# A recurrent attention and a three-branch MLP in one program: chunks 0 to 3 select on VectorE alone, clears after the warming operand's, weight loads after x's copies, and another order of the first part's attention steps

## The chip, the cores and the metric

The program runs on one core of one Trainium2 chip. Time is device time in microseconds (us); where several runs are given, their median counts. Profiled rows come from one execution, whose own time is given below.

## What is computed

The reference, cut to what matters (batch 4, 8 heads, 768 tokens, head size 48; the MLP has model size 384 and inner size 768; the four MLP weights arrive as 64-bit floats):

```
for t in range(S):
    cur = einsum('bhd,bhe->bhde', u[None] * k[t], v[t])
    y[t] = einsum('bhd,bhde->bhe', r[t], state + cur)
    state = w[t][..., None] * state + einsum('bhd,bhe->bhde', k[t], v[t])
x = y.transpose(0, 2, 1, 3).reshape(3072, 384)
h = maximum(maximum(x @ w1, x @ w2), x @ w3)
out = h @ w_out
```

## The kernel before

**Tiling.** Each of the 4 sequences is cut into 6 chunks of 128 tokens, 24 chunks in all, numbered k. Four chunks make a half of 512 tokens, which is one tile `x` of the MLP, 6 halves in all. A guard at the end (`judge`, a flag, a slow general program behind a branch) covers inputs for which the fast form is not exact; it plays no part here.

**Attention steps.** `steps` (line 574) names each step of a chunk with a letter; a string of such letters with chunk numbers is the order in which every engine gets its instructions, since the schedule is manual and each engine runs its list in order:

- n: load `tin` (w, r, k, u of a chunk, L250) on SP. b, s, f, r: backward scan (VectorE, L357) and a copy of its ends (ScalarE, L359), reciprocal (L365), forward scan (L370), products that scale k and r (L381, L382). c: a guard's square (ScalarE, L387).
- d, D, e: the diagonal. For chunks 0 to 5 VectorE multiplies r and k (L395), TensorE sums against u (L408), ScalarE copies the sums (`cs`, L421). Then for chunks 0 and 1 ScalarE writes eight scaled identities into the weight tile `a` (L429), for the others GpSimd selects them in (L432). From chunk 6 on the product is GpSimd's (L398, L399) and the sum VectorE's (L423). e also issues the next chunk's `v` and `kr` loads on SP (L237, L238).
- X: scores into the PSUM tile `gram` (L453). N: `take_full`, ScalarE copies the third block of `gram` to `a` (L464). M: `take`, VectorE copies the other two blocks under a mask (L468). O: `take_alone`, VectorE does both (L472, then L468).
- T, U, S, R: transposed k (L483, copied to `kn` by ScalarE, L485), state update (L506, L510), its scaling (ScalarE L522 for chunks 0 to 3, VectorE L519 and L525 later), the state's share of y (L496).
- V, Z: the two groups of value products into `y` (L545). E: ScalarE copies `y` into `x` (L563); for the third and fourth chunk of the first half, and for the last chunk of any later half, six small copies within `x` follow (`x<-x`, L572), three on SP and three on ScalarE's queue in the first half, all six on SP later.

**MLP.** `moe_groups` yields groups. A half has 18 input groups (6 blocks f of the inner size, 3 branches) and 8 output groups of three matmuls 128x384 each. In the first half the first 6 input groups are plain fp32 products against weights 0 to 5 (`psm<-x,wh`; the first two are begun on 384 tokens, L149, and finished on 128, L157), and the other 12 take three fp32r products each (`x_hi,wh`, `x_lo,wh`, `x_hi,wl`, L169); its output groups are plain (L189). `take_up` drains each PSUM tile: ScalarE copies the first branch (L132), VectorE takes the maximum with the other two (L135). Three PSUM tiles serve the groups.

**Weights.** There are 24 weight tiles. `load_w` loads one as raw 64-bit words (384 KB, L306, SP, six raw buffers). `begin` casts the top part on ScalarE (`split_w1`, L313) and first loads until `NST` tiles are ahead of the cast; `weights` (letter c) joins the parts on VectorE (`split_w2`, L320); `fix` (letter f) splits a weight into a high part on ScalarE (L112) and a low part on VectorE (L113).

**Order.** `FRONT` (line 72) is the order of the opening: attention steps of chunks 0 to 3 and parts of 4, with W (warming matmuls on a tile `warm`, L594), w (one weight load), i (a cast), p and m (an MLP group), c, x, y (splitting x). `START` (line 80) follows: m is a group, a is one unit of the attention strings `TURN` and `ORD` (a chunk has 6 units; the first of a chunk holds R, V, U, the next chunk's X, Z and E), c a weight, f a split. It ends with the first input group of the second half. After it a loop keeps groups and units in step, which is unchanged. Before all, `warmer(WARM)` issues ten warming matmuls; GpSimd clears three `top` tiles (L287) before it clears `warm` (L589).

```
def take_alone(k):
    to, data = views(k)
    nc.vector.tensor_copy(out=to[:, :, 2, :], in_=data[:, :, 2, :])
    take(k)
...
while loaded < min(NW, begun + (NST if groups else 1)):
    load_w()
```

Of the kernel before, what the change touches and what calls it, by code (L numbers as in the profile page):

```python
# [62 lines left out]
GPH = 3 * FT + 2 * CPH  # L63
UPC = 6
UPH = UPC * CPH
NST = 4
WARM = 10
XD, LEAD = -2, 0

FRONT = ("b0 s0 f0 d0 W2 D0 W3 r0 X0 N0 e0 T0 W3 c0 b1 s1 d1 D1 U0 f1 W2 R0 e1 S0 M0 V0 Z0 E0 n3 r1 "
# [3 lines left out]
TURN = "b1 d1 w | f1 w | D1 r1 c1 | e1 M0 w | "  # L76
ORD = "w R0 V0 U0 X1 Z0 E0 N1 b2 d2 | f2 n3 w | D2 S0 r2 c2 | e2 M1 w | T1 w | |"


START = ("mcyamcyfamcyffamcfamcfamcfamcfamcfamcfamcfamcfamcfamcfcamccamccamaamaamaamafafaxmafmmammaaf")  # L80
CS = 6
EARLY = 2
LINE = 128
# [12 lines left out]
def kernel(ctx: ExitStack, tc, tin, nat, u_flat, u_pair, v_t, w_all, out, ytr):  # L96
    nc = tc.nc
# [107 lines left out]
    with ExitStack() as fast:  # L205
# [77 lines left out]

        stage = {}
        tops = [cst.tile([128, PC], U32, name=f"top{i}") for i in range(3)]
        for t in tops:
            nc.gpsimd.memset(t[:, :], 0)  # L287

        loaded = 0

# [5 lines left out]
        def load_w():  # L296
            nonlocal loaded
            if loaded == NW:
                return
            i, loaded = loaded, loaded + 1  # L300
            if w_all.dtype == F32:
                place(i)
                nc.sync.dma_start(out=wval[i], in_=w_all[i])
                return
            raw = raw_p.tile([128, lines(2 * PC + 1)], I32, name="raw")
            nc.sync.dma_start(out=raw[:, :].bitcast(U16)[:, 1:4 * PC + 1], in_=w_all[i].bitcast(U16))  # L306
            stage[i] = raw
# [271 lines left out]
        def ahead(step, k):  # L579

            if k < NK and (step, k) not in ready:
                ready.add((step, k))
                steps[step](k)
# [3 lines left out]
            nc.vector.tensor_copy(out=ident2[lo:lo + HC, :], in_=ident[lo:lo + HC, lo:lo + HC])  # L587
        warm = cst.tile([128, 128], BF16, name="warm")
        nc.gpsimd.memset(warm[:, :], 0.0)  # L589

        def warmer(n):
            wps = ps_m.tile([128, HT], F32, name="psm")
            for _ in range(n):
                nc.tensor.matmul(wps[:, :], lhsT=warm[:, :], start=True, stop=True,  # L594
                                 rhs=warm[:, :].unsqueeze(1).broadcast_to([128, HT // 128, 128]))
# [49 lines left out]
        def begin():  # L645

            nonlocal begun
            while loaded < min(NW, begun + (NST if groups else 1)):
                load_w()
# [74 lines left out]
        def take_x(early=False):  # L724
            h = len(xs)
            there = ("E", CPH * (h + 1) - 2) in ready if early else units >= min(UPH * (h + 1) + XD, UPC * NK)
            if h < NH and there and groups >= GPH * h - 2 * CPH:
                x_parts(h)
# [43 lines left out]
        simple = dict(p=part, a=unit, c=weights, i=begin, w=load_w, m=group, f=fix, y=x_next, x=lambda: take_x(True))  # L772
        for step in FRONT.split():
            if step in simple:
# [3 lines left out]
            else:  # L778
                ahead(step[0], int(step[1:]))
        for step in START:  # L780
            simple[step]()
# [7 lines left out]
    with tc.If(verdict[0] != 0, label="general"), ExitStack() as slow:  # L789
        pool = lambda name, bufs, **kw: slow.enter_context(tc.tile_pool(name=name, bufs=bufs, **kw))  # L790
        c1 = pool("c1", 1)
# [83 lines left out]
        with tc.For_i(0, NH) as half:  # L875
            x = xs_p.tile([128, KT, HT], F32, name="x")
# [73 lines left out]
```

## Time and profile before

| what | us |
|---|---|
| median of 3 runs | 419.01 |
| lowest and highest run | 413.47, 419.7 |
| the profiled execution's time | 419.3 |
| its span, first to last instruction | 417.5 |

A row of a timeline gives start, duration, engine, line, operation, output and inputs, and a count; what stands in brackets is the engine's idle time before it and what ended that. Rows with a count merge neighbours. PEclk is the granted clock of TensorE as a share of its full 2.4 GHz, so 0.50 is 1.2 GHz. Weight loads into TensorE (PEld) overlap its matmuls.

### The profile page before, as it was taken

The page shows a single profiled execution, that of the slowest core. Times are in us where ns is not written, and L with a number is a line of the kernel's source. Part 1 is how long each engine was busy: PE and PEld are TensorE (multiplying, and loading weights), DVE is VectorE, ACT ScalarE, POOL GpSimd, SP SyncE. Part 2 cuts the span into 40 slices and gives each one's busy share as a digit, 9 for nine tenths or more (in the row PEclk, how much of TensorE's full clock was granted, in tenths as well). Part 3 has the DMA queues.
Part 4 walks back from the last instruction along what each step waited for, and adds up shares of the span by engine and source line. Part 5 has one row for each costly group of instructions (what it writes and reads, how often), then busy time and mean ns, then how long its engine had stood idle before and what let it go on. Part 6 is the DMA issues. An engine that isn't in the chain of part 4 may idle for free.

```text
span 417.5 us, 9220 instructions
## 1 busy us (share of the span) xinstructions
PE 400.6 (96%) x3762; PEld 325.6 (78%) x3762; DVE 251.2 (60%) x437; ACT 179.1 (43%) x406; POOL 82.0 (20%) x95
## 2 busy tenths in 40 slices
PE   5899899999699999999999999999999999999995
PEld 2666558776387888988889988888988888978894
DVE  7666789989637776547758558667636523223310
ACT  1744674844424323447447656545623321412211
POOL 3030104324221213321312311321321300000000
PEclk9769999999989999999999999999999999999998
DMA  8544888671361303190312280430470000300002
GB/s 223 168 147 139 252 320 276 188 228 42 86 203 36 125 5 121 50 289 6 125 57 68 61 271 14 147 102 0 111 233 3 2 2 0 96 1 2 0 1 79
DMA packets 20814, 44.65 MB, mean 107 GB/s; under 512 B 2944, under 2 KB 9536, under 8 KB 20768
## 3 DMA queue, kind: packets, MB, share of 16 engines
q1 hardware_dynamic: 20160, 43.34, 33.3%
q10 hardware_dynamic: 608, 0.69, 0.6%
q8 instruction: 30, 0.49, 0.5%
q14 instruction: 16, 0.13, 0.1%
HBM read 38.12 MB, written 4.72 MB: 103 GB/s over the span
## 4 chain that ended last, share of the span: by engine, by line
PE 82%; DVE 6%; DMA 4%; ACT 3%; issue 2%; POOL 1%; ACTq 1%; SPq 0%; POOLq 0%; DVEq 0%
PE psm L169 47%; PE psm L189 17%; PE gram L453 4%; PE y L545 4%; PE tu L506 3%; PE y L496 3%; DMA raw<-in_w_all_dram 2%; PE psm L594 2%; PE tu L483 2%; DMA x<-x 2%; DVE wl L113 1%; DVE wl L320 1%; DVE h_hi L135 1%; DVE tin L381 1%; PE psm L408 1%
## 5 line engine op out<-in xcount | busy, mean ns | idle before, releaser
L169 PE MATMUL psm<-x_hi,wh 128*128 128x512 f32 x306 | 122.7, 401 | 3.5 <-ACT m L200 3.2
L169 PE MATMUL psm<-x_hi,wl 128*128 128x512 f32 x306 | 120.1, 393 | 0.7 <-DVE wl L113 0.7
L169 PE MATMUL psm<-x_lo,wh 128*128 128x512 f32 x306 | 119.9, 392 | 0.0
L135 DVE TENSOR_TENSOR m<-psm,m 128x512 f32<-128x512 f32 x60 | 41.5, 691 | 74.0 <-PE psm L169 62.3
L169 PEld LDWEIGHTS psm<-x_hi,wh 128*128 128x128 f32 x306 | 57.8, 189 | 16.9 <-ACT m L200 3.9
L169 PEld LDWEIGHTS psm<-x_hi,wl 128*128 128x128 f32 x306 | 57.8, 189 | 13.7 <-DVE wl L113 1.5
L169 PEld LDWEIGHTS psm<-x_lo,wh 128*128 128x128 f32 x306 | 57.9, 189 | 11.4 <-DVE x_lo L113 0.2
L432 POOL TENSOR_SCALAR_AFFINE_SELECT a<-cs 64x512 f32<-64x512 f32 x44 | 31.6, 718 | 138.3 <-DVE cs L423 52.1
L189 PE MATMUL psm<-wl,h_hi 128*128 128x384 f32 x168 | 56.5, 379 | 0.0
L398 POOL TENSOR_TENSOR kr<-kr 128x384 f32<-128x384 f32 x18 | 25.0, 1391 | 109.4 <-PE y L545 101.4
L563 ACT COPY x<-y 112x512 f32<-112x512 f32 x24 | 14.1, 586 | 68.2 <-PE y L545 68.2
L189 PE MATMUL psm<-wh,h_hi 128*128 128x384 f32 x120 | 41.0, 342 | 0.0
L189 PE MATMUL psm<-wh,h_lo 128*128 128x384 f32 x120 | 40.2, 335 | 0.0
L112 ACT CAST h_hi<-m 128x512 fp32r<-128x512 f32 x30 | 18.7, 622 | 47.9 <-DVE m L135 47.9
L189 PEld LDWEIGHTS psm<-wl,h_hi 128*128 128x128 f32 x168 | 31.4, 189 | 5.6
L387 ACT ACTIVATE gf<-gf 112x1034 f32<-112x1034 f32 x24 | 25.6, 1068 | 22.3 <-DVE tin L382 22.3
L113 DVE TENSOR_TENSOR h_lo<-m,h_hi 128x512 fp32r<-128x512 f32 x30 | 20.7, 690 | 21.8 <-ACT h_hi L112 21.8
L357 DVE TENSOR_TENSOR_SCAN gf<-tin,d_bwd 112x517 f32<-112x517 f32 x24 | 30.6, 1274 | 3.7 <-DMA tin<-in_tin_dram 3.7
L370 DVE TENSOR_TENSOR_SCAN gf<-tin,d_fwd 112x517 f32<-112x517 f32 x24 | 31.7, 1320 | 0.7
L545 PE MATMUL y<-a,v 64*48 64x64 f32 (+3 forms) x768 | 26.4, 256 | 0.8
L545 PEld LDWEIGHTS y<-a,v 64*64 64x64 f32 (+1 forms) x768 | 22.4, 132 | 4.7 <-issue 1.8
L113 DVE TENSOR_TENSOR x_lo<-x,x_hi 128x512 fp32r<-128x512 f32 x18 | 11.6, 689 | 22.6 <-ACT x_hi L112 22.6
(87 smaller groups left out, 508.0 us busy)
## 6 DMA issues: line engine op xcount, KB each, us to landing
tin<-in_tin_dram SPq DMA_DIRECT2D x23, 448.0 KB, 4.6
raw<-in_w_all_dram SPq DMA_DIRECT2D x24, 384.0 KB, 5.7
kr<-in_nat_dram SPq DMA_DIRECT2D x18, 384.0 KB, 4.9
tin<-in_tin_dram SPq DMA_DIRECT2D x23, 231.0 KB, 2.9
v<-in_nat_dram SPq DMA_DIRECT2D x24, 192.0 KB, 4.7
out_dram<-m SPq DMA_DIRECT2D x23, 192.0 KB, 2.1
x<-x SPq DMA_DIRECT2D x30, 32.0 KB, 2.0
tin<-in_tin_dram SPq DMA_DIRECT2D x1, 256.0 KB, 4.8
```

Source lines behind the costliest of these rows:

```text
L112: nc.scalar.copy(out=hi, in_=src)
L113: rest = lambda: nc.vector.tensor_tensor(out=lo, in0=src, in1=hi.bitcast(F32), op=ALU.subtract)
L135: nc.vector.tensor_tensor(out=m[:, :], in0=ps[:, :], in1=m[:, :], op=ALU.max)
L169: nc.tensor.matmul(ps[:, :], lhsT=wt[f * 3 + wi][:, ct * 128:(ct + 1) * 128], rhs=xt[:, ct, :], start=(n == 0), stop=(n == KT * len(terms) ...
L189: nc.tensor.matmul(pss[tt][:, 0:DM], lhsT=ht[f][:, tok], rhs=wt[FT * 3 + f][:, :], start=(f == 0 and i == 0), stop=(f == FT - 1 and i == l ...
L357: nc.vector.tensor_tensor_scan(out=gf[0:112, 0, ::-1], data0=t[0:112, 0:WC][:, ::-1], data1=d_bwd[0:112, ::-1], initial=0.0, op0=ALU.mult, ...
L370: nc.vector.tensor_tensor_scan(out=gf[0:112, 1, :], data0=tbuf[k % NB][0:112, 0:WC], data1=d_fwd[0:112, :], initial=0.0, op0=ALU.mult, op1 ...
L387: nc.scalar.activation(out=flat, in_=flat, func=AF.Square, accum_out=acc[0:112, k:k + 1])
L398: nc.gpsimd.tensor_tensor(out=n[:, 0, :], in0=n[:, 0, :], in1=n[:, 1, :], op=ALU.mult)
L432: nc.gpsimd.affine_select(out=a[rows, 0:2, :, :], pattern=[[0, 2], [0, 4], [1, HC]], in_=cs[rows, :].rearrange("p (a b) -> p a b", a=2).un ...
L453: nc.tensor.matmul(to, lhsT=p["kp"][q:q + 48, pr, lo:lo + HC], rhs=p["rp"][q:q + 48, pr, HC * late:C], start=(hh, lo) not in begun, stop=T ...
L545: mm = nc.tensor.matmul(p["y"][64 * half:64 * half + m, hh, j, HC * late:C], lhsT=natt[k][0][lo:lo + HC, h * D:h * D + m], rhs=a[:, j, :] ...
```

## The change

Chunks 0, 1 and 2 get O where they had N and M, as chunk 3 had already: VectorE does both copies, and ScalarE's copy (L464) is gone for them. Two weight loads (w w) move from behind E2 to behind E3. `NST` goes from 4 to 3. The three clears of `top` follow the clear of `warm` on GpSimd. `START` has the same number of groups (24), units (28) and weights (18), in another order: units come earlier among the three-product groups, so that the second half's x is written seven output groups ahead of its first product and not four; two more splits (f) stand in it, 19 for 17.

```
-NST = 4
+NST = 3
-FRONT = ("b0 s0 f0 d0 W2 D0 W3 r0 X0 N0 e0 T0 W3 c0 b1 s1 d1 D1 U0 f1 W2 R0 e1 S0 M0 V0 Z0 E0 n3 r1 "
-         "W1 X1 N1 d2 D2 e2 w w T1 c1 b2 s2 R1 U1 S1 M1 V1 Z1 E1 f2 r2 "
-         "W4 X2 N2 d3 D3 e3 w n4 w T2 c2 b3 s3 R2 U2 S2 i i M2 V2 Z2 E2 w w f3 r3 "
-         "W3 X3 T3 i R3 O3 x V3 Z3 E3 n5 U3 p p d4 w c n6 w m D4 b4 s4 c c3 S3 m w f4 c e4 m r4 c X4 N4 T4 R4 c4 w w")
+FRONT = ("b0 s0 f0 d0 W2 D0 W3 r0 X0 e0 T0 W3 c0 b1 s1 d1 D1 U0 f1 W2 R0 e1 S0 O0 V0 Z0 E0 n3 r1 "
+         "W1 X1 d2 D2 e2 w w T1 c1 b2 s2 R1 U1 S1 O1 V1 Z1 E1 f2 r2 "
+         "W4 X2 d3 D3 e3 w n4 w T2 c2 b3 s3 R2 U2 S2 i i O2 V2 Z2 E2 f3 r3 "
+         "W3 X3 T3 i R3 O3 x V3 Z3 E3 w w n5 U3 p p d4 w c n6 w m D4 b4 s4 c c3 S3 m w f4 c e4 m r4 c X4 N4 T4 R4 c4 w w")
-START = ("mcyamcyfamcyffamcfamcfamcfamcfamcfamcfamcfamcfamcfamcfcamccamccamaamaamaamafafaxmafmmammaaf")
+START = ("mcyamcyfamcyffamcfamcfamcfaamcfamcfaamcfamcfaamcfamcfaamcfamccaamccamcaaamfamfmfamxfamamfmamf")
...
         tops = [cst.tile([128, PC], U32, name=f"top{i}") for i in range(3)]
-        for t in tops:
-            nc.gpsimd.memset(t[:, :], 0)
...
         nc.gpsimd.memset(warm[:, :], 0.0)
+        for t in tops:
+            nc.gpsimd.memset(t[:, :], 0)
```

In the changed program the lines from 288 to 589 stand two lines higher, so that L470 below is L472 of before, L466 is L468, L570 is L572 and so on.

VectorE, chunk 0's selection and chunk 1's preparation, before:

```order
L370 SCALAR_TENSOR_TENSOR gf<-tin_118,d_fwd 112x517
L468 COPY_PREDICATED a<-mask,gram 128x2x2x128
L381 TENSOR_TENSOR tin_118<-tin_118,gf 112x2x128 x2
L382 TENSOR_TENSOR tin_118<-tin_118,gf 112x512
L395 TENSOR_TENSOR kr<-tin_119 112x2x128 x2
```

The same place now:

```order
L368 SCALAR_TENSOR_TENSOR gf<-tin_118,d_fwd 112x517
L470 COPY a<-gram 128x256
L466 COPY_PREDICATED a<-mask,gram 128x2x2x128
L379 TENSOR_TENSOR tin_118<-tin_118,gf 112x2x128 x2
L380 TENSOR_TENSOR tin_118<-tin_118,gf 112x512
L393 TENSOR_TENSOR kr<-tin_119 112x2x128 x2
```

One copy is added on VectorE ahead of the selection, and nothing else moves; chunks 1 and 2 have the same.

SP's queue at the end of the first half's attention, from chunk 4's `tin` (n4, tin_118) to chunk 5's (tin_119), before:

```order
L250 DMA tin_118<-in_tin_dram 112x528
L306 DMA raw<-in_w_all_dram 128x1536
L572 DMA x<-x 16x384 x3
L306 DMA raw<-in_w_all_dram 128x1536 x2
L572 DMA x<-x 16x128 x3
L250 DMA tin_119<-in_tin_dram 112x528
```

The same place now:

```order
L250 DMA tin_118<-in_tin_dram 112x1024
L304 DMA raw<-in_w_all_dram 128x1536
L570 DMA x<-x 16x384 x3
L570 DMA x<-x 16x128 x3
L304 DMA raw<-in_w_all_dram 128x1536 x2
L250 DMA tin_119<-in_tin_dram 112x528
```

Weights 4 and 5 now stand behind both sets of x's copies.

TensorE from the last value products of chunk 7 (they end the second half's x) to the second half's first product, before:

```order
L545 MATMUL y<-a,v 64x64
L545 MATMUL y<-a,v 48x64
L189 MATMUL psm<-wl,h_hi 128x384 x12
L169 MATMUL psm<-x_hi,wh 128x512
L169 MATMUL psm<-x_lo,wh 128x512
```

The same place now:

```order
L543 MATMUL y<-a,v 64x64
L543 MATMUL y<-a,v 48x64
L189 MATMUL psm<-wl,h_hi 128x384 x15
L481 MATMUL tu<-ident,tin_119 128x112 x4
L189 MATMUL psm<-wl,h_hi 128x384 x6
L169 MATMUL psm<-x_hi,wh 128x512
```

Twenty-one output matmuls (seven groups) stand there now, where twelve (four groups) stood.

## Rows read from the trace of the kernel before

**Rows 1.** The page's first part: busy time, share of the span, instructions of each engine.

```profile
PE 400.6 (96%) x3762; PEld 325.6 (78%) x3762; DVE 251.2 (60%) x437; ACT 179.1 (43%) x406; POOL 82.0 (20%) x95
```

**Rows 2.** The chain that ended last, in order of time: start, us, what.

```profile
2.97 1.08 POOL top L287 x3
...
140.08 8.39 PE psm L169 x36
```

**Rows 3.** Timeline of TensorE alone, 0 to 50 us.

```profile
14.22 0.67 PE L506 MATMUL tu<-v,kn 128*64 128x48 f32 x16 [1.29 <-ACT kn L485]
...
17.84 1.56 PE L453 MATMUL gram<-tin 48*64 48x128 f32 x32
...
27.89 1.34 PE L453 MATMUL gram<-tin 48*64 48x128 f32 x32
...
33.96 0.90 PE L453 MATMUL gram<-tin 48*64 48x128 f32 x32
...
38.40 4.04 PE L149 MATMUL psm<-x,wh 128*128 128x384 f32 x12
...
43.54 1.07 PE L157 MATMUL psm<-x,wh 128*128 128x128 f32 x6 [1.10 <-DMA x<-x]
...
45.10 0.94 PE L157 MATMUL psm<-x,wh 128*128 128x128 f32 x6
...
48.54 0.90 PE L453 MATMUL gram<-tin 48*64 48x128 f32 x32
```

**Rows 4.** Stretches: length, busy time by engine (x instructions), PEclk, DMA share, GB/s.

```profile
15.50:28.50 13.00, 12.76 (x171) 9.05 (x174) 8.27 (x14) 6.80 (x24) 2.28 (x2) 0.50 0.34 105
64.24:78.96 14.72, 14.45 (x122) 11.51 (x123) 14.65 (x27) 8.32 (x18) 4.29 (x4) 1.00 0.70 220
115.00:120.00 5.00, 5.00 (x20) 3.99 (x19) 1.06 (x1) 1.90 (x4) 0.00 (x0) 0.74 0.72 236
```

**Rows 5.** VectorE's groups from 0 to 39 us: busy us, mean ns, idle before.

```profile
L357 DVE TENSOR_TENSOR_SCAN gf<-tin,d_bwd 112x517 f32<-112x517 f32 x5 | 6.1, 1229 | 1.5 <-DMA tin<-in_tin_dram 1.5
L370 DVE TENSOR_TENSOR_SCAN gf<-tin,d_fwd 112x517 f32<-112x517 f32 x4 | 5.1, 1268 | 0.0
L381 DVE TENSOR_TENSOR tin<-tin,gf 112x256 f32<-112x256 f32 x8 | 4.3, 573 | 0.0
L395 DVE TENSOR_TENSOR kr<-tin 112x256 f32<-112x256 f32 x10 | 3.7, 412 | 0.0
L468 DVE COPY_PREDICATED a<-mask,gram 128x512 f32<-128x512 int32 x4 | 2.9, 732 | 7.8 <-ACT a L464 5.9 <-ACT a L429 1.8
L382 DVE TENSOR_TENSOR tin<-tin,gf 112x512 f32<-112x512 f32 x4 | 2.7, 684 | 0.0
...
L472 DVE COPY a<-gram 128x256 f32<-128x256 f32 x1 | 0.4, 425 | 1.5 <-PE gram L453 1.5
```

**Rows 6.** Timeline of all engines, round chunk 7's y and the second half's first product.

```profile
103.05 8.01 PE L189 MATMUL psm<-wl,h_hi 128*128 128x384 f32 x24
...
114.30 0.79 PE L169 MATMUL psm<-x_hi,wh 128*128 128x512 f32 x1 [3.24 <-ACT m L200]
```

**Rows 7.** Timeline of all engines, 10 to 45 us: VectorE, SP's queue and ScalarE.

```profile
10.77 1.23 DVE L370 TENSOR_TENSOR_SCAN gf<-tin,d_fwd 112x517 f32<-112x517 f32 x1
...
34.56 1.86 SPq L572 DMA_DIRECT2D x<-x  x3
...
42.21 0.62 ACT L313 CAST top<-raw 128x384 f16<-128x384 bf16 x1
```

**Rows 8.** The tile `raw` from 0 to 60 us: issue of a weight load to its landing.

```profile
DMA to landing us min/median/max: 3.5/6.3/8.4
```

**Rows 9.** VectorE's groups from 64.24 to 78.96 us.

```profile
L113 DVE TENSOR_TENSOR wl<-wl,wh 128x384 fp32r<-128x384 f32 x7 | 5.1, 730 | 0.0
L320 DVE SCALAR_TENSOR_TENSOR wl<-raw,top 128x384 uint32<-128x384 uint32 x6 | 3.7, 616 | 0.0
L135 DVE TENSOR_TENSOR h_hi<-psm,h_hi 128x512 f32<-128x512 f32 x4 | 2.7, 669 | 0.0
```

## The prediction

> **What bounds the kernel now.** I read the page first, then the chain that ended last in order of time, then TensorE's own timeline, stretches with the granted clock, and VectorE's groups. The page says that TensorE is busy 96% of the span and VectorE 60% [rows 1]. From about 118 us on the chain is TensorE's groups one behind another, 36 fp32r matmuls in 8.39 us [rows 2], that is 2.10 us for a group of nine; the change leaves these groups as they are. So a gain must come from the part before. There the reader is to see four places.
>
> First, the scores of chunks 1, 2 and 3 start at 17.84, 27.89 and 33.96 us [rows 3]: 10.05 us from the one to the next, then 6.07. In the long gap TensorE works at 0.50 of its clock, 1.2 GHz, for 13 us on end [rows 4], and not long before that it had stood still 1.29 us for `kn` [rows 3]. VectorE meanwhile loses 7.8 us in front of its masked copies, waiting for ScalarE's copy (5.9) and for the diagonals (1.8) [rows 5]. Second, TensorE waits 1.10 us for x's second set of copies at 43.54 [rows 3]. Third, from 64.24 to 78.96 both engines are full: TensorE 14.45 and VectorE 14.65 of 14.72 us [rows 4]. Fourth, the second half's first product comes at 114.30 after 3.24 us of idle time [rows 6], and then the clock shows 0.74 in 115 to 120 [rows 4].
>
> **The change part by part.** The sum is made against the profiled execution's 419.3 us (span 417.5); the median of the runs is 419.01, so the two agree to 0.3.
>
> *The clears.* The three clears of `top` take 1.08 us ahead of the warming operand [rows 2]. Behind it, the warming matmuls end about 1.1 us sooner. VectorE's scans set what comes next, so I count nothing; GpSimd's next work is chunk 2's selection, and the clears' first reader is the first weight's cast, both far later. Without that cover it would be 1.1 us, either way.
>
> *N and M become O.* ScalarE loses three copies, VectorE gains three of 0.43 us. With ScalarE's copy gone from the front of its queue, the eight scaled identities of chunk 0 follow the diagonal's sum at once and are done before VectorE is, so VectorE runs without the 7.8 us of waits. By durations [rows 5] one chunk costs it 1.23 and 1.27 (scans), 2 x 0.57 and 0.68 (products), 2 x 0.41 (diagonal), 0.43 and 0.73 (selection): 6.3 us. Its forward scan of chunk 1 starts at 10.77 and takes 1.23 [rows 7], so it is free at 12.0. Selecting chunk 0 (1.16) and scaling chunk 1 (1.83) gives the scores of chunk 1 at 15.0; one round later those of chunk 2 at 21.3, and those of chunk 3 at 27.6, against 33.96: 6.4 us sooner. TensorE must do a chunk in 6.3 us for that. It did one in 6.07 at full clock and needed 10.05 at the low one [rows 3]. I take the full clock, since `kn` of chunk 0 is now copied about when the matmuls ahead of its reader end, so that the 1.29 us of idle time should go; that it doesn't is the first rival. From the scores of chunk 3 to the first MLP product it is 4.44 us (33.96 to 38.40) [rows 3], with ScalarE's queue issuing x's first set in between as before, so that product starts at 32.0. Term: -6.4. Bounds: 3.5 us less if the low clock stays (below), and about 1 more if the instructions overlap at their ends.
>
> *x's copies ahead of the loads.* The second set no longer queues behind 768 KB of weights. The 1.10 us wait goes: -1.1. The bounds are 0, if the set is late for its issue alone, and -1.1.
>
> *The two loads behind.* They are issued when the second set is: at 32.0 plus the 1.86 us that three copies take on SP [rows 7], 33.9. In before they stood ahead of it. A weight lands 3.5 to 8.4 us after its issue, 6.3 in the median [rows 8]; as the queue is nearly empty here I take 4.0. So weight 4 is cast at 37.9. In ScalarE's list that cast stands ahead of the first branch's drain, and in VectorE's list weight 4 stands ahead of the scaling of chunk 4: behind the wait stand the scores of chunk 4 and all that follows. In before it was 6.33 us from the cast (42.21) [rows 7] to these scores (48.54) [rows 3], but 0.9 of it was a wait for products that ended at 46.04 [rows 3] and now end first; 5.4 are left. The scores of chunk 4 come at 43.3, 5.2 us sooner than before, where the two terms above promise 7.5. Term: +2.3. Bounds: 0, if the landing takes the least and ScalarE is late anyway, and +4.6 with the median landing.
>
> *NST.* One load less stands ahead of a cast. SP's queue is then held less by full raw buffers, which helps tin and x; TensorE pays only if a weight lands late. I count 0; the price is in the last rival.
>
> *START.* The end first. Chunk 7's y is done when the last 12 output matmuls begin, at 103.05 [rows 6], and from there to the second half's first product it took 11.25 us: copies, ScalarE's casts, VectorE's parts. Now 21 output matmuls stand there. Twelve took 8.01 us, so 21 take 14.0, more than 11.25. The 3.24 us of idle time go. So does the stretch at the low clock behind them, which in 115 to 120 cost a clock of 0.74 for 5 us, that is 1.3 us, and some more in 114 to 115: I take 1.7. Terms: -3.2 and -1.7. Next late is the rest of the splits, which VectorE then has 2.8 us to do. Bounds: 0 and -5.
>
> The price stands earlier. Units of chunks 4 to 7 come every 4 groups and not every 6, over 11 groups, so 2.75 chunks stand where 1.8 stood. Six groups and a chunk took VectorE 14.65 us, of which its work for the groups is (5.1 + 3.7 + 2.7) / 6 = 1.92 us a group [rows 9]. With two groups less a chunk takes VectorE 14.65 - 3.83 = 10.8, and TensorE 14.72 - 2 x 2.10 = 10.5. VectorE is late by 0.3 per chunk, 0.8 over 2.75; with what is lost where a selection comes just too late I take +1.0. Bounds: 0 (the lead of one split that START keeps hides it) and +4.8.
>
> That upper bound comes from GpSimd. In the same stretch GpSimd is busy 4.29 us in four instructions [rows 4], and if all of it held VectorE up, it would be in the groups' durations though it belongs to the chunk: (11.5 - 4.29) / 6 = 1.2 us a group, so 14.65 - 2.4 = 12.25 against 10.5, 1.73 late per chunk, 4.8 in all. The Trainium skill, SBUF — State Buffer, section "SBUF: two separate sides", speaks for this end: GpSimd and a VectorE instruction with two SBUF inputs share a port pair as an exclusive lock, and the loser stands for the whole instruction. By that rule the sum would be 3.8 us worse. The row gives VectorE 14.65 busy of 14.72 either way and cannot tell, and since GpSimd's selections write more than they read I stay near the lower end.
>
> **Sum:** -6.4 - 1.1 + 2.3 - 3.2 - 1.7 + 1.0 = -9.1, so 419.3 - 9.1 = 410.2 us.
>
> **The rivals.** *The clock falls in the first part again.* For: the trace shows 13 us at 0.50 [rows 4] in just this work, and one of the three runs took 413.47, which such a chance would explain. Against: the idle time ahead of it should be gone. Then from chunk 1's scores (15.0) to chunk 2's it takes 10.05 again and not 6.3, 3.75 us more: 414.0.
>
> *VectorE becomes the bound of the three-product groups.* For: it is full there already [rows 4]. Against: a lead of one split. With +4.8 in place of 1.0: 414.0.
>
> *Nothing of the price shows.* Weight 4 lands in time and VectorE keeps up: 2.3 and 1.0 come off, 406.9. For: the least landing is 3.5 [rows 8], and VectorE's instructions overlap. Against: ScalarE's order puts five pieces of work behind that cast.
>
> *The loads come late, and it ends slower than before.* With NST 3 a weight's load is issued three groups ahead of its cast and not four: 3 x 2.45 = 7.4 us (14.72 / 6 a group) [rows 4]. A landing above that holds ScalarE's queue, and the twelve three-product groups behind it each wait for the difference. From 8.2 us on (12 x 0.8 = 9.6) it eats the whole gain; at the 8.4 of the slowest load [rows 8] on all of them it is 12 x 1.0, 422.2, slower than before. Against: the median is 6.3, and the units add loads of their own ahead of need.
>
> **How the numbers follow.** Forecast 410.2: 0.50, from 407.5 to 412.5 by itself. Low clock 414.0: 0.22. VectorE 414.0: 0.09. No price 406.9: 0.15. Late loads 422.2: 0.04. The range leaves out the last case and the tails of the others: 405.5 (no price, and 1 us from overlap) to 415.5 (one of the 414.0 cases with 1.5 us of the other bounds). About 2%, that is 410.6 us, is what a measurement of this kernel can tell from no change. The forecast stands at that edge: 0.32 of its 0.50 lie below it, with the 0.15 of no price and 0.03 of the others that makes 0.50 for faster by over 2%; 0.03 for slower by over 2%, from the late loads; 0.47 between.
>
> **What would show it.** Right: no wait of the masked copy on ScalarE in chunks 0 to 2; scores of chunks 1 to 3 near 15, 21 and 28 us, at full clock between; no wait on x's copies before 40 us; a wait of ScalarE for weight 4 and TensorE idle ahead of chunk 4's scores; the second half's first product near 105 to 106 without idle time or low clock ahead of it; VectorE full and TensorE with small gaps in the three-product groups. Wrong: a clock of 0.50 in the first 30 us; casts that wait for landings in every group; half a dozen TensorE waits on VectorE there; or a new wait ahead of the second half, on the splits or on PSUM.

## The result and the profile after

| | before | after |
|---|---|---|
| median of 20 runs, us | 418.99 | 412.53 |
| lowest and highest run, us | 413.47, 422.83 | 410.29, 415.78 |
| profiled execution, us (span) | 419.3 (417.5) | 415.78 (414.0) |
| its mean granted clock | 0.976 | 0.984 |

The ratio of the runs is 0.9887, with an interval of 0.9851 to 0.9922: about 1.1% faster. By the medians the gain is 6.5 us, or 1.5%. The two differ because the kernel before has two kinds of runs: five of its 20 took 413.5 to 414.6 us and most of the others about 419. The ratio goes by averages (about 417.5 and 412.7 us over the runs that it counts), while the median of before lies among its longer runs. The forecast was 410.2 us; the median lies in its range and 2.3 us above it. The forecast gave 0.50 to a gain of more than 2% and 0.47 to a smaller change; the smaller one came.

Single runs of one kernel lie several us apart, and a run's time goes with the mean clock that it was granted: runs of the kernel before took 413.4 us at 0.989 and 418.8 at 0.977, runs of the kernel after 410.4 at 1.000 and 415.0 at 0.985. Runs more than 1.5% above their kernel's fastest are left out of every ratio, so the first experiment, where five of six runs are such, has none. The profiled execution of after is the longest of its 20 runs, so its rows show more loss than a usual run has.

First TensorE's timeline of the kernel after: start, us, engine, line, operation, count, and in brackets the idle time in front and what ended it.

```profile
14.84 0.90 PE L451 MATMUL gram<-tin 48*64 48x128 f32 x32
...
20.69 0.90 PE L451 MATMUL gram<-tin 48*64 48x128 f32 x32
...
26.33 0.90 PE L451 MATMUL gram<-tin 48*64 48x128 f32 x32
...
30.25 0.67 PE L504 MATMUL tu<-v,kn 128*64 128x48 f32 x16 [0.60 <-ACT kn L483]
...
31.27 4.04 PE L149 MATMUL psm<-x,wh 128*128 128x384 f32 x12
...
40.07 5.49 PE L169 MATMUL psm<-x,wh 128*128 128x512 f32 x6 [2.67 <-ACT h_hi L132]
45.49 1.14 PE L451 MATMUL gram<-tin 48*64 48x128 f32 x32
...
82.78 0.50 PE L169 MATMUL psm<-x_hi,wh 128*128 128x512 f32 x1 [2.07 <-ACT h_hi L132]
...
98.02 0.56 PE L543 MATMUL y<-a,v 64*64 64x128 f32 x16 [1.89 <-issue]
...
114.02 0.69 PE L169 MATMUL psm<-x_hi,wh 128*128 128x512 f32 x1
```

Against [rows 3] the scores of chunks 1, 2 and 3 come at 14.84, 20.69 and 26.33 instead of 17.84, 27.89 and 33.96, and the first MLP product at 31.27 instead of 38.40: 7.1 us sooner. Of that, 3.05 us are left at the scores of chunk 4 (45.49 for 48.54), and 0.28 at the second half's first product (114.02 for 114.30). There, however, nothing stands still any more, where [rows 6] had 3.24 us of idle time. The idle time now stands at 40, 82 and 98 us.

The stretches of after (length, busy time by engine, then the clock, the DMA share, GB/s):

```profile
15.50:28.50 13.00, 12.63 (x282) 9.05 (x275) 11.46 (x21) 8.16 (x25) 4.27 (x4) 1.00 0.73 210
40.00:45.00 5.00, 4.93 (x6) 1.85 (x6) 3.38 (x5) 1.20 (x4) 1.40 (x2) 0.50 1.04 274
...
80.00:90.00 10.00, 7.93 (x100) 6.06 (x99) 7.94 (x15) 5.91 (x14) 3.69 (x4) 0.83 0.66 208
...
110.00:120.00 10.00, 10.00 (x83) 7.27 (x81) 5.60 (x10) 2.88 (x7) 1.52 (x2) 1.00 0.27 99
```

The 13 us that stood at 1.2 GHz [rows 4] are at 2.4 GHz. TensorE does 282 matmuls there, where it did 171. But the clock is at 0.50 from 40 to 45, right behind the 2.67 us of idle time, so the six products there take 5.49 us, against 2.74 at full clock in experiments below. It is low again behind the idle time at 82.

The masked copy among VectorE's groups from 0 to 39 us, whose wait was 7.8 us in [rows 5]:

```profile
L466 DVE COPY_PREDICATED a<-mask,gram 128x512 f32<-128x512 int32 x4 | 2.9, 728 | 0.0
```

And the chain around the new wait (start, us, what):

```profile
33.54 3.59 DMA raw<-in_w_all_dram
...
37.64 0.98 ACT gf L385
...
38.69 0.85 ACT sstar L520 x4
39.54 0.48 ACT h_hi L132
...
40.07 5.49 PE psm L169 x6
```

This is the wait that the prediction named: weight 4's load goes out at 33.54 (33.9 forecast) and takes 3.59 us to its cast (4.0 forecast). Behind the cast in ScalarE's list stand a guard's square, four scalings of the state and, last, the drain of the first branch, whose PSUM buffer TensorE needs.

### The profile page after: what moved, and what is told of

It is laid out like the page before. It is cut to its first block, busy times and chain, and to the rows that moved or that the text cites. A ratio compares the mean times of both kernels' runs of the same rounds, so it can differ in the third digit from the quotient of the medians.

```text
span 414.0 us, 9214 instructions
## 1 busy us (share of the span) xinstructions
PE 397.9 (96%) x3762; PEld 322.8 (78%) x3762; DVE 253.6 (61%) x440; ACT 177.9 (43%) x403; POOL 82.7 (20%) x95
## 4 chain that ended last, share of the span: by engine, by line
PE 88%; DVE 4%; ACT 2%; DMA 2%; issue 2%; ACTq 1%; SPq 1%; POOL 0%; POOLq 0%; DVEq 0%
PE psm L169 51%; PE psm L189 19%; PE gram L451 4%; PE y L543 4%; PE tu L504 3%; PE y L494 3%; PE psm L594 2%; PE tu L481 2%; DMA raw<-in_w_all_dram 2%; DVE wl L113 1%; DVE gf L355 1%; PE psm L406 1%; DVE h_hi L135 1%; ACTq L570 1%; SPq L570 1%
## 5 line engine op out<-in xcount | busy, mean ns | idle before, releaser
L368 DVE TENSOR_TENSOR_SCAN gf<-tin,d_fwd 112x517 f32<-112x517 f32 x24 | 33.2, 1382 | 0.7
L543 PE MATMUL y<-a,v 64*48 64x64 f32 (+3 forms) x768 | 25.4, 248 | 2.6 <-issue 1.9
L543 PEld LDWEIGHTS y<-a,v 64*64 64x64 f32 (+1 forms) x768 | 21.4, 128 | 6.3 <-issue 4.5
L132 ACT COPY m<-psm 128x512 f32<-128x512 f32 x30 | 17.4, 581 | 18.6 <-PE psm L169 12.8
```

What stands on the lines that cost most here:

```text
L132: nc.scalar.copy(out=top["m"][:, :], in_=ps[:, :])
L368: nc.vector.tensor_tensor_scan(out=gf[0:112, 1, :], data0=tbuf[k % NB][0:112, 0:WC], data1=d_fwd[0:112, :], initial=0.0, op0=ALU.mult, op1 ...
L543: mm = nc.tensor.matmul(p["y"][64 * half:64 * half + m, hh, j, HC * late:C], lhsT=natt[k][0][lo:lo + HC, h * D:h * D + m], rhs=a[:, j, :] ...
```

## The experiments

Two questions were open. Is the first part faster because VectorE no longer waits, or because TensorE's clock no longer falls? And where does the rest go? Each kernel ran beside the kernel before on the same chip (medians of before 418.8 to 419.1). The ratios hold within a round only: runs of before near 414 us were 9 of 23 in one round, 6 of 23 in the next and none of 11 in the last, that of e5, e10, e11 and e12. From one round to another the text compares medians.

### The first part

**The selection undone.**

```
-... X0 e0 T0 ... S0 O0 V0 ... X1 d2 ... S1 O1 V1 ... X2 d3 ... O2 V2 ...
+... X0 N0 e0 T0 ... S0 M0 V0 ... X1 N1 d2 ... S1 M1 V1 ... X2 N2 d3 ... M2 V2 ...
```

> Chunks 0 to 2 select as before (ScalarE's copy, then VectorE's masked copy), all else as in the changed kernel. Theory A (the selection on VectorE alone gives the first part's 6 to 7 us): the scores of chunks 2 and 3 come 4 us or more later than the changed kernel's 20.7 and 26.3 us, VectorE waits again for ScalarE in front of the masked copies (some 6 us in all), and the time is 4 to 7 us above the changed kernel's median of 412.5, near that of the kernel before. Rival B (the sooner warming operand and the clock at full speed behind it do it): those scores come within 2 us of 20.7 and 26.3, and the time rises by less than 2 us.

Median 422.18 us, lowest run 414.09 at a mean clock of 0.992, the others 421.2 to 423.2 at 0.968. TensorE's timeline of the profiled run (423.19 us):

```profile
13.65 0.67 PE L504 MATMUL tu<-v,kn 128*64 128x48 f32 x16 [1.29 <-ACT kn L483]
...
26.93 1.56 PE L451 MATMUL gram<-tin 48*64 48x128 f32 x32
```

And its stretch from 15.50 to 28.50 us:

```profile
15.50:28.50 13.00, 12.88 (x173) 9.23 (x175) 7.72 (x13) 6.25 (x22) 2.29 (x2) 0.50 0.40 128
```

The wait for `kn` is back, 1.29 us to the hundredth, and so are the clock of 0.50, the late scores of chunk 2 (26.93) and 7.1 us of VectorE's waits ahead of the masked copies. In this run rival B's early scores are not there. But the median is 9.7 us above the changed kernel's, beyond theory A's 4 to 7, and as the kernel has no ratio it proves nothing; what the run shows is where to look: at that wait and the clock.

**The kernel before with its idle time filled.** Six matmuls on `warm` where TensorE waits for `kn`.

```
-... D1 U0 f1 W2 ...
+... D1 W6 U0 f1 W2 ...
```

> The kernel before, with six more warming matmuls where TensorE stands still 1.29 us for kn of chunk 0; they compute nothing that is read. Theory A (the first part of the kernel before is slow because that idle time is followed by 13 us at half the clock): the granted clock stays at 1.00 from 15 to 28 us, the scores of chunk 2 come near 24 us instead of 27.9, and the median falls from 419 to 413 to 415.5. Rival B (the selection's way over ScalarE and VectorE sets these scores, and the low clock beside it costs little): the scores of chunk 2 within 1.5 us of 27.9 and the median within 1.5 us of 419.

Median 414.33 us, ratio 0.9925 (0.9883 to 0.9967), all twelve runs between 411.8 and 416.0. TensorE's timeline, the scores of chunks 2 and 3:

```profile
22.69 0.90 PE L453 MATMUL gram<-tin 48*64 48x128 f32 x32
...
28.33 0.90 PE L453 MATMUL gram<-tin 48*64 48x128 f32 x32
```

The same stretch as above, now at full clock:

```profile
15.50:28.50 13.00, 12.58 (x282) 9.03 (x282) 11.21 (x19) 10.63 (x37) 4.33 (x4) 1.00 0.64 192
```

And the masked copy among VectorE's groups from 0 to 39 us:

```profile
L468 DVE COPY_PREDICATED a<-mask,gram 128x512 f32<-128x512 int32 x4 | 2.9, 734 | 3.0 <-ACT a L429 1.9 <-ACT a L464 1.1
```

Theory A holds. Matmuls that compute nothing make the kernel before 4.5 us faster, with ScalarE still in the selection. The scores of chunk 2 come 5.2 us sooner than in [rows 3], and VectorE's waits shrink from 7.8 us [rows 5] to 3.0: the other 4.8 us were waits for products that came late because TensorE ran at 1.2 GHz. The filled kernel's time is that of the shorter runs of the kernel before (413.5 to 414.6 us among its 20; like runs beside the experiments had clocks near 0.989). So the fall may stay out in those runs by itself; no trace of one was taken.

**The selection alone**, in the kernel before (the first edit's + and - exchanged).

> The kernel before with the selection of chunks 0 to 2 on VectorE alone and nothing else of the change. Theory A (this edit carries nearly all of the gain, through the idle time for kn that it takes away and the clock that stays up): the scores of chunks 2 and 3 come near 21 and 27 us, the granted clock stays at 1.00 in the first 40 us, the median is 412 to 414.5, and the runs near 422 that the kernel before shows are gone. Rival B (the clears and the order START, not the selection, carry it): the median at 416 or above.

Median 411.94 us, ratio 0.9822 (0.9784 to 0.9860), runs from 411.1 to 414.1. The stretch:

```profile
15.50:28.50 13.00, 12.70 (x294) 9.21 (x283) 11.07 (x19) 9.33 (x30) 4.28 (x4) 1.00 0.69 210
```

Scores of chunks 2 and 3 at 21.85 and 27.48, full clock, no run near 422. Theory A, with a median 0.06 us below its bounds: one edit of the five brings 7.1 us against the usual runs of before, all that the whole change brings and a little more. By the medians 4.5 us come with the filler alone, which keeps the clock up, and this kernel is 2.4 us below the filled one. Of those 2.4 the two profiles show 0.85 at the scores of chunk 3 (27.48 for 28.33) and 0.76 at the second half's first product (107.66 for 108.42); the rest is not located.

**The clears ahead again.**

```
+for t in tops:                          (ahead of `loaded = 0`)
+    nc.gpsimd.memset(t[:, :], 0)
...
-for t in tops:                          (behind the clear of `warm`)
-    nc.gpsimd.memset(t[:, :], 0)
```

> The changed kernel with the three clears ahead of the warming operand again. Theory A (the clears cost nothing where they stood, since VectorE's scans set the first scores): warming starts about 1.1 us later, the first scores stay within 0.3 us, time within 0.8 us of 412.5. Rival B (they delay the start by their 1.08 us, or let the clock fall): scores of chunk 1 about 1 us later than 14.84 and the time 1 us or more above 412.5.

Median 413.58 us (411.67 to 415.82), 1.05 above the changed kernel's, but the two sets of runs overlap almost wholly. In its profile the scores of chunk 1 come at 15.24, 0.40 later than in after's. Theory A's bounds are missed by a little on both counts, and rival B's shift of 1 us is not there. Some shift is: with the clears behind, the nine profiles that also have the new selection show these scores at 14.29 to 14.94, with the clears ahead the two show 15.24 and 16.00 (the second in the selection alone). What that costs in the end, between 0 and 1 us, stays open.

### The two loads

**The loads between x's sets again**, all else as in the changed kernel.

```
-... Z2 E2 f3 r3 ... Z3 E3 w w n5 ...
+... Z2 E2 w w f3 r3 ... Z3 E3 n5 ...
```

> The two loads stand between x's two sets of copies again, all else as in the changed kernel. Theory A (their delay costs the 2.67 us of idle time in front of chunk 4's scores and the low clock behind it): ScalarE's cast of weight 4 waits for no transfer, TensorE doesn't stand still for 2 us between 37 and 42, the clock stays at 1.00 there, the scores of chunk 4 come at 42 to 43.5 instead of 45.5, a wait of about 1 us on x's second set is back at most, and the time is 1 to 4 us lower (408.5 to 411.5). Rival B (the wait only changes its name: x's copies, or the drain, hold the same scores): chunk 4's scores within 1 us of 45.5, time within 1 us of 412.5 or above it.

Median 410.37 us (409.52 to 411.08, six runs), ratio 0.9851 (0.9785 to 0.9916): 2.2 us below the changed kernel. TensorE's timeline:

```profile
35.81 1.11 PE L157 MATMUL psm<-x,wh 128*128 128x128 f32 x6 [0.45 <-DMA x<-x]
...
38.19 2.74 PE L169 MATMUL psm<-x,wh 128*128 128x512 f32 x6
40.86 0.90 PE L451 MATMUL gram<-tin 48*64 48x128 f32 x32
...
77.92 0.50 PE L169 MATMUL psm<-x_hi,wh 128*128 128x512 f32 x1 [2.06 <-ACT h_hi L132]
...
91.76 0.56 PE L543 MATMUL y<-a,v 64*64 64x128 f32 x16 [2.03 <-issue]
```

Theory A, with the scores of chunk 4 at 40.86, sooner than its 42 to 43.5. The wait that the edit was to take away is only 0.45 us now, not the 1.10 of [rows 3]; the wait that it brought takes 2.67 us in the profile of after, and sometimes the clock. Beside the rest of the change, this edit is a loss.

**The wait filled.** Ten matmuls on `warm` in front of the waiting group, into `gram`'s buffer.

```
-... f4 c e4 m r4 ...
+... f4 c e4 G10 m r4 ...
...
+def filler(n):
+    wps = ps_g.tile([128, 2, HT], F32, name="gram")[:, 0, :]
+    for _ in range(n):
+        nc.tensor.matmul(wps, lhsT=warm[:, :], start=True, stop=True,
+                         rhs=warm[:, :].unsqueeze(1).broadcast_to([128, HT // 128, 128]))
```

> The changed kernel, with ten warming matmuls (2.1 us) in the 2.67 us in which TensorE waits in front of chunk 4's group; they write a PSUM buffer that nobody reads then. The wait on weight 4 stays as it is. Theory A (most of what the delayed loads cost is the clock behind the wait): the clock stays at 1.00 from 40 to 46 us, the six products behind the wait take 2.74 us and not 5.49, the scores of chunk 4 come at 42.5 to 43.5, the median is 410 to 411.5, and no run is above 414. Rival B (the wait itself is the cost): the median within 0.7 us of 412.5.

TensorE's timeline of the profiled run:

```profile
36.55 2.32 PE L600 MATMUL gram<-warm 128*128 128x512 bf16 x10
39.20 2.84 PE L169 MATMUL psm<-x,wh 128*128 128x512 f32 x6 [0.32 <-ACT h_hi L132]
42.23 0.90 PE L451 MATMUL gram<-tin 48*64 48x128 f32 x32 [0.19 <-DVE tin L380]
```

The profiled run (410.68 us, mean clock 1.000) is as theory A had it, the scores at 42.23. The median is not: 412.47 us, the changed kernel's own, with one run at 414.33. By the medians rival B holds: to fill the wait brings nothing. The wait itself puts these scores 1.37 us behind those of the kernel above (42.23 against 40.86), less than the 2.1 us between the two medians. The five other runs had mean clocks of 0.989 to 0.994; where they lost theirs was not traced. Without the filler the low clock behind the wait comes often and not always: of the four such profiles with the new selection, after shows 0.50 from 40 to 45 us, the ones with NST 4 and with START back 0.66, the one with the clears ahead 1.00.

**The loads earlier still**, right behind weight 3's.

```
-... w n4 w T2 ... Z3 E3 w w n5 ...
+... w n4 w w w T2 ... Z3 E3 n5 ...
```

> The changed kernel with the two loads right behind weight 3's, ahead of both of x's sets. Theory A (any place in which the weight has landed before 37 us will do): no wait on weight 4, time within 0.7 us of e2_loads_back's 410.37, TensorE's 0.45 us wait on x's second set gone or moved to the first set. Rival B (x's first set now queues behind 768 KB of weights and the first MLP product is late by 1 us or more): 411.5 to 413.

Median 410.66 us (409.24 to 413.20). Theory A: no wait on weight 4, and the short wait on x moves to the first set (0.41 us at 31.89). The runs can't tell this place from the old one; what both have is that the weight is there in time.

### NST

```
-NST = 3
+NST = 4
```

> NST 4 again, all else as in the changed kernel. Theory A (with a load less ahead, weights land late in the three-product groups and hold ScalarE's casts, which hold VectorE and TensorE): the waits of the joins on the casts of 0.8 us near 96 and 3.0 us near 91 are gone, TensorE's 1.9 us near 98 shrinks, and the time is 1 to 3 us lower (409.5 to 411.5). Rival B (the loads are late because SP's queue is held by something else, or the waits are covered): those waits stay and the time is within 1 us of 412.5.

Median 412.78 us (411.0 to 416.45). Rival B: no effect that these runs can tell. The wait of 1.9 us ahead of chunk 7's values is not made by one load less; TensorE is busy for 8.08 of the 10 us from 90 to 100 here and for 8.11 in the changed kernel.

### START

**START as before**, with the changed kernel's loads (first), and with the loads between x's sets (second).

```
-START = "mcyamcyfamcyffamcfamcfamcfaamcfamcfaamcfamcfaa...
+START = "mcyamcyfamcyffamcfamcfamcfamcfamcfamcfamcfamcfa...
```

> START as before, all else as in the changed kernel. Theory A (the other order is worth about the 4 us that were forecast for it): TensorE stands still 2 to 4 us in front of the second half's first product, with a low clock behind it, the stalls of 2.0 us near 81 and 1.9 us near 98 are gone, and the time is 2 to 5 us higher (414.5 to 417.5). Rival B (what it takes from the end it gives back in the three-product groups): time within 1 us of 412.5, or lower.

> The changed kernel with the two loads between x's sets (as in e2_loads_back) and START as before. Theory A (the new order is worth 2 to 2.5 us whatever the loads do, as 414.79 against 412.53 had it): 412 to 413.5, TensorE idle some 3 us ahead of the second half. Rival B (the order was worth that only beside the delayed loads): within 0.7 us of e2_loads_back's 410.37.

The first: median 414.79 us (411.94 to 417.38), 2.3 above the changed kernel, within theory A's 2 to 5. The second: 411.69 (411.20 to 412.74), 1.3 above the kernel with the loads back; no run of the one lies among the runs of the other, but the median is in neither theory's range. So the order is worth something, but less than the 3.9 us of the forecast and, in the second pair, less than theory A's 2. What TensorE waited for in e11_loads_start (engine, line, waited for: us, times, longest):

```profile
PE psm L169 <- ACT m L200: 3.6, 1, 3.6
PE psm L594 <- POOL warm L587: 3.2, 1, 3.2
PE psm L169 <- DVE wl L113: 0.7, 1, 0.7
```

The same view of the kernel with the new order, e2_loads_back:

```profile
PE psm L594 <- POOL warm L587: 3.2, 1, 3.2
PE psm L169 <- ACT h_hi L132: 2.1, 1, 2.1
PE y L543 <- issue: 2.0, 1, 2.0
```

Leave out the start-up wait of 3.2 us that both have. With the old order 3.6 + 0.7 = 4.3 us of idle time stand ahead of and behind the second half's first product; with the new one 2.1 + 2.0 = 4.1 us stand further ahead, the first in the three-product groups, the second behind the first two output groups. The idle time was moved, not removed. From the scores of chunk 4 to the second half's first product the old order took 66.10 us (39.97 to 106.07) and the new one 66.90 (40.86 to 107.76). What the new order gains in these two profiles stands behind that product: with the old one the clock is low there (e11_loads_start),

```profile
106.00:112.00 6.00, 5.93 (x16) 4.80 (x17) 1.84 (x2) 1.81 (x6) 0.76 (x1) 0.50 0.62 197
```

and with the new one it is 1.000 over the whole span. That shorter pieces of idle time are the reason is not shown: in the profile of e3_start_back 3.23 us of idle time at 110 were followed by full clock, and in that of after 2.07 us at 82 by a low one.

**GpSimd's products taken out** for chunks 6 and 7, on top of the loads' old place.

```
-CS = 6
+CS = 8
```

> The two loads back between x's sets (as in e2_loads_back), and chunks 6 and 7 also take their diagonals from VectorE's products and TensorE's sums, so that GpSimd's two products of 1.2 to 1.8 us each fall out for these chunks. Theory A (GpSimd's products lengthen VectorE's instructions beside them: the subtraction of 0.55 us takes 1.0 to 1.4 and the scan of 1.23 us takes 2.04, and VectorE is the bound from 50 to 100 us): VectorE gets two products of 0.41 us per chunk and loses a sum of 0.54 us and some 1.5 us of stretch, scans beside these chunks take 1.23 us again, TensorE's wait of 2.06 us near 76 us shrinks to under 1 us, and the time is 1 to 2.5 us below e2_loads_back's 410.4. Rival B (ScalarE's order makes the waits, not VectorE's load): time within 0.7 us of 410.4.

VectorE's backward scans from 50 to 100 us, in e2_loads_back:

```profile
L355 DVE TENSOR_TENSOR_SCAN gf<-tin,d_bwd 112x517 f32<-112x517 f32 x4 | 6.5, 1629 | 0.0
```

and in this kernel:

```profile
L355 DVE TENSOR_TENSOR_SCAN gf<-tin,d_bwd 112x517 f32<-112x517 f32 x4 | 4.9, 1223 | 0.0
```

TensorE's timeline of this kernel, its two longer waits:

```profile
75.78 0.50 PE L169 MATMUL psm<-x_hi,wh 128*128 128x512 f32 x1 [0.80 <-ACT h_hi L132]
...
91.97 0.56 PE L543 MATMUL y<-a,v 64*64 64x128 f32 x16 [1.89 <-issue]
```

And its stretch from 90 to 100 us:

```profile
90.00:100.00 10.00, 8.11 (x92) 5.95 (x89) 9.14 (x16) 2.84 (x8) 5.77 (x4) 0.66 0.07 16
```

The mechanism is there: the scan takes 1.22 us instead of 1.63 in the mean, the subtraction of a weight 0.63 instead of 0.76, and the wait near 76 us shrinks from 2.06 to 0.80. So GpSimd's products do lengthen VectorE's instructions; in the changed kernel one scan that begins at 74.82, with 0.95 us of such a product still to run, takes 2.04 us and not 1.23. That agrees with the rule of the Trainium skill, SBUF — State Buffer, section "SBUF: two separate sides", that the two share a port pair. The time is not lower, though: 412.38 us (410.85 to 413.87), 2.0 above e2_loads_back. The wait of 1.89 us ahead of chunk 7's values is untouched, and in this profile the clock behind it is 0.66. Theory A fails on the time, and so does rival B, which had it within 0.7 us. Where VectorE's relief went, its joins of weights show; 50 to 100 us, first e2_loads_back, then this kernel:

```profile
L318 DVE SCALAR_TENSOR_TENSOR wl<-raw,top 128x384 uint32<-128x384 uint32 x15 | 9.0, 602 | 1.6 <-ACT top L311 1.6
L318 DVE SCALAR_TENSOR_TENSOR wl<-raw,top 128x384 uint32<-128x384 uint32 x15 | 8.9, 594 | 4.3 <-ACT top L311 4.3
```

VectorE now waits 2.7 us longer for ScalarE's casts. The wait ahead of chunk 7's values, for which the profile names no releaser ("issue"), stands at the end of a chain over both engines. In the changed kernel:

```profile
94.52 1.07 ACT L385 ACTIVATE gf<-gf 112x1034 f32<-112x1034 f32 x1 [3.07 <-DVE tin L380]
...
95.58 1.15 ACT L311 CAST top<-raw 128x384 f16<-128x384 bf16 x2
...
96.27 0.56 DVE L318 SCALAR_TENSOR_TENSOR wl<-raw,top 128x384 uint32<-128x384 uint32 x1 [0.78 <-ACT top L311]
...
97.21 0.72 DVE L466 COPY_PREDICATED a<-mask,gram 128x512 f32<-128x512 int32 x1
```

A guard's square on ScalarE waits for VectorE's scaling, the casts stand behind the square, VectorE's join waits for them, and the masked copy that writes the values' operand `a` stands behind the join. It ends at 97.93, and the values begin at 98.02; in e2_loads_back, e4_nst4 and this kernel the two are 0.10 us apart as well. The wait near 76 us (82 in the changed kernel) has the same head: the square stands ahead of the drain for which TensorE waits. That the waits go when the square stands later was not tested.

**The two waits filled**, on top of the loads' old place: `k` in START stands for eight matmuls on `warm` into `y`'s buffer, written like the filler above.

```
-... mcfaamcfamccaamccamcaaamf ...
+... mcfaakmcfamccaamccamcaakamf ...
```

> e2_loads_back with eight warming matmuls (1.8 us) in each of the two places where TensorE still stands still about 2 us, in front of chunk 6's group near 76 us and of chunk 7's values near 90 us; they write y's buffer before it is used and nobody reads that. Theory A (what is left of the spread between runs is the clock behind these two waits): mean granted clock 0.995 or more in all runs, median 409.0 to 410.0, highest under 410.5. Rival B (fillers delay the work behind them as much as they save, or the clock falls elsewhere): median 410.4 or above, spread of 1.5 us as before.

Median 409.39 us (408.65 to 410.64), ratio 0.9759 (0.9724 to 0.9795); mean clock 0.997 to 1.000 in all six runs. What TensorE waited for:

```profile
PE psm L594 <- POOL warm L587: 3.2, 1, 3.2
PE tu L504 <- ACT kn L483: 0.9, 1, 0.9
PE psm L157 <- DMA x<-x: 0.5, 1, 0.5
PE psm L169 <- ACT h_hi L132: 0.3, 1, 0.3
```

Median and clock are as theory A had them, but for one run 0.14 us above its bound. The spread is not: 2.0 us, against 1.6 without the fillers, with 410.23 us at a clock of 1.000 and 408.65 at 0.998. So what spread is left is not the clock, and the 1.0 us to e2_loads_back, whose runs overlap these, is not beyond doubt. This kernel's median is 3.1 us below the changed one's and 9.6 below that of before.

## Why the prediction was right, and where it was not

**A sum of the parts.** By the medians the way from 419.0 to 412.5 is: the selection -7.1 (e10_sel_alone); clears and NST together -0.25 (from there to e11_loads_start); START -1.3 (from there to e2_loads_back); the loads +2.2 (from there to the changed kernel). These are differences of medians from three rounds, and they depend on the order: taken the other way, the loads cost 3.1 beside the old START (from e11_loads_start to e3_start_back) and START gives 2.3 beside the new loads. The forecast had -6.4, 0, -3.9 and +1.2 (+2.3 - 1.1). So the first part gave 0.7 us more than forecast and the clears 0.25, START gave 2.6 less and the loads cost 1.0 more: together the 2.6 us by which 6.5 is less than 9.1.

**N and M become O, -6.4: right in size.** Scores were forecast at 15.0, 21.3 and 27.6 and came at 14.84, 20.69 and 26.33; the full clock was a condition of the term and was kept. The weight lay elsewhere than the step put it. It told the gain as VectorE's 7.8 us of waits that go, and the clock as the condition beside it. The runs show that 4.5 of the 7.1 us come from keeping the clock up alone, and that most of those waits were its effect. The wait of `kn` went for the reason that the step gave: ScalarE's copy N0 no longer stands ahead of it.

**x's copies, -1.1: oversized.** With the loads in their old place the wait is 0.45 us once the rest of the first part is sooner (e2_loads_back), and with the selection alone there is none (e10_sel_alone), so there was less than half of it to win.

**The two loads behind, +2.3: the mechanism to the letter, the net cost too small.** Issue, landing and the queue behind the cast were as forecast. The scores of chunk 4 were forecast at 43.3: they came at 42.80 in e8_clears_back, where the clock stayed up behind the wait, and at 45.49 in after, where it fell, which the step did not think of; that made 5.49 us out of 2.74. By the medians the net cost is 2.2 for the 1.2 of the forecast, and 0.65 of that difference is the oversized term above.

**START, -3.2 - 1.7 + 1.0: this step failed.** The first two terms came: no idle time at 114 and full clock in 110 to 120. The third was "VectorE is late by 0.3 per chunk, 0.8 over 2.75; with what is lost where a selection comes just too late I take +1.0". What stands there is 4.1 us of idle time, near the upper bound of 4.8; with 4.1 in place of 1.0 the step's sum is -0.8, beside the -1.3 measured. VectorE is busy for 48.2 of the 50 us from 50 to 100 with the new order (e2_loads_back), and was for 38.0 of the 40 us from 50 to 90 with the old one (e11_loads_start), so there was little room for more work. The rival "VectorE becomes the bound" had the right place and about the right size, but a part of the mechanism only. The experiment without GpSimd's products shows that they lengthen VectorE's work and the first of the two waits; the second stays, and VectorE then waits for ScalarE. In the step VectorE's load alone set the price; the rows show VectorE and ScalarE waiting for each other in turn, round the guard's square.

**The place.** The second half's first product was forecast near 105 to 106 and came at 114.02 in a run 3.3 us above the median. With the wait at 40 filled and full clock throughout (e7_after_fill) it came at 109.12, so 3 to 4 us of this miss are there without any low clock.

**The clears and NST, 0 and 0.** The times can't tell either from nothing; the clears may be worth up to 1 us, and the scores of chunk 1 do come sooner with them behind, so VectorE's scans do not hide all of it.

**The other rivals.** The clock did not fall in the first 39 us; it fell at 40, where no rival had it. The late landings of the last rival did not come: in the profile of after no cast from 50 to 100 us waits for a landing. VectorE waits for two casts, near 91 and 96 us, but these are held by ScalarE's own list, and a load more ahead of them changes nothing that can be measured.

**One table shows what the profiled executions are made of.** For each profiled execution, the span times (1 - mean granted clock) is what the low clock would have taken from an engine that is busy throughout; so the column is an upper bound, worked out and not measured.

| kernel | span | clock | span x (1 - clock) | the rest |
|---|---|---|---|---|
| before | 417.5 | 0.976 | 10.0 | 407.5 |
| before, wait filled | 413.0 | 0.989 | 4.5 | 408.5 |
| selection alone | 410.5 | 0.994 | 2.5 | 408.0 |
| after | 414.0 | 0.984 | 6.6 | 407.4 |
| after, START back | 411.8 | 0.992 | 3.3 | 408.5 |
| after, loads back | 407.7 | 1.000 | 0.0 | 407.7 |
| loads back, two waits filled | 407.9 | 0.998 | 0.8 | 407.1 |

The spans differ by 9.8 us, the rest by 1.4. Over all fourteen profiled executions it is 13.7 and 2.5, the rest going from 406.5 (e11_loads_start) to 409.0 (e7_after_fill, at a clock of 1.000). So most of what separates these executions goes with the clock. "The rest" is a lower bound and was not measured: two runs of after at a clock of 1.000 had spans of 408.6 and 408.9, over a microsecond above its 407.4.

## What to carry to other kernels

Where TensorE's clock falls behind a short wait, price the wait with the stretch behind it: 1.29 us of idle time cost the kernel before 4.5 us in its usual runs, and six matmuls that compute nothing bought them back. Before work is moved on an engine that is full over a whole stage, ask what it pushes out; idle time that leaves one place comes back in another (4.3 us became 4.1). And a transfer moved out of one reader's way has its own reader: look up what stands behind that one in its engine's list.

## What was not expected of the hardware

- 1.29 us of idle time of TensorE were followed by 13 us at 1.2 GHz, in the kernel before [rows 3, 4] and again in the first experiment. Such a fall does not come every time: 2.06 and 2.03 us of idle time in e2_loads_back were followed by full clock (mean 1.000 over the span), 1.89 us in e9_loads_diag by 0.66 from 90 to 100 us. The length of the idle time alone does not decide it: 3.23 us in e3_start_back were followed by full clock from 110 to 115 us, 3.61 us in e11_loads_start by 0.50 from 106 to 112.
- A change of 7.1 us in the first part's end left only 0.28 us at 114 us in the profiled runs; the medians differ by 6.5 us all the same. With runs of one kernel 5 to 10 us apart, one profile against one profile tells where time is lost, not how much.
